# Attention units: the second bank of the even head's transposed probabilities is copied by VectorE, between the two maxima

## The chip, the cores and the metric

The kernel runs on one core of one Trainium2 chip. The metric is the device time of one launch in microseconds (us): the median of several runs. A core has TensorE (PE, and PEld for its weight loads), VectorE (DVE), ScalarE (ACT), GpSimd (POOL) and DMA queues that SyncE (SP) issues; each works through its own queue in order, and semaphores order the engines among each other.

## The reference, cut to what matters

```python
scores = scale * np.matmul(q, k.transpose(0, 1, 3, 2))      # B=2, H=8, S=576, D=64
scores = scores + bias.transpose(2, 0, 1)[None, :, :, :]
scores = scores - np.max(scores, axis=-1, keepdims=True)
attn = np.exp(scores)
attn = attn / (np.sum(attn, axis=-1, keepdims=True) + 1e-09)
return np.matmul(attn, v).astype(np.float32)
```

The bias comes from a small network over relative positions. Behind the attention stand a layer `max(x@w1, x@w2, x@w3) @ w_out` and a layer of 8 gated experts, each `max(x@w1, 0) @ w2`.

## The kernel before, in words

The kernel makes the bias first and stores it to DRAM, then does the attention, then the two layers. The change is in the attention alone.

The attention goes over 4 pairs of heads, p = 0 to 3, and in each over 9 units, k = 0 to 8: 36 units, u = 0 to 35. A unit is 128 query rows of one batch (k = 8: 64 rows of each batch) for both heads of the pair, the even head x = 0 and the odd head x = 1. All the work is issued by one hand-written loop over s = 0 to 35, and each engine takes its share in the order of that loop:

- `u_qk(s)` (lines 459 to 482): the score matmuls of unit s, into two PSUM tiles `sc`, one for each head, two banks each. The pool has two such tiles in all, so the next unit writes the same ones. The first pair multiplies unsplit inputs (line 470); the other three pairs split q and k into high and low parts and do three products (line 481), with the matmuls of the two heads in turn, the even head first. A unit with k = 8 has twice as many.
- `u_tr(s - 1, 0)` and `u_tr(s - 1, 1)` (lines 535 to 542): the transposes of the previous unit's probabilities, even head and odd head. Each goes to two PSUM tiles `pt`, one bank each: the first 64 rows to bank 0, the other 64 to bank 1. There are only these two banks, which even and odd head use in turn, so `u_tr(s - 1, 1)` waits until both banks of the even head have been copied.
- `pv_part(s)` (lines 624 to 628): matmuls of transposed probabilities with v, for units further back. Steps k = 2 and 4 of a pair have half as many again as the others.
- `u_max(s, x)` (lines 487 to 498): VectorE adds the bias to the scores of one head and takes the maximum; it shows as the instruction of line 494 with a short accumulator read behind it. It reads an `sc` tile, and so frees it.
- `u_exp(s, x)` (lines 500 to 506): ScalarE's exponential of one head.
- `u_ev(s - 1, x)` (lines 544 to 559): copies the two `pt` banks of one head to SBUF (`pts`), from where `pv_part` takes them. Before the change ScalarE (line 557) copies both banks of the even head and bank 1 of the odd head; VectorE (line 559) copies bank 0 of the odd head.
- Behind these come the pieces that only some units have: `pv_ev` and `r_add` on VectorE, and a step of weight preparation (`w_step`) at the s of `W_AT` (7 to 10, 18 to 20, 27 to 33). In the first units the loop adds spare matmuls on TensorE (`busy`, line 221).

The last unit's transposes stand behind the loop (lines 676 to 696).

Of the kernel before, what the change touches and what calls it, by code (L numbers as in the profile page):

```python
# [52 lines left out]
def make_body(stop=None):  # L53
    def body(tc, a):
# [21 lines left out]
        with ctx, tc.manual_schedule():  # L76
# [66 lines left out]
            def load_item(n):  # L143
                if n < len(w_items):
                    kind, i = w_items[n]
                    w_raw[n] = load_w64(a[f"moe_w{i % 3 + 1}"][i // 3] if kind == "w"
                                        else a["moe_w_out"][128 * i:128 * i + 128], n)
# [67 lines left out]
            def busy(p, to, n):  # L215

                q, kk = (t[:, 0] for t in qk_t[p])
                for _ in range(n):
                    for x in range(2):
                        h = slice(64 * x, 64 * x + 64)  # L220
                        T.matmul(out=to[x][:, :SH], lhsT=q[h, :128], rhs=kk[h, :SH], start=True, stop=True)
# [223 lines left out]
            with ExitStack() as actx:  # L445
# [10 lines left out]
                NP, NU = H // 2, 9 * H // 2  # L456
                un = {}

                def u_qk(u):
                    p, k = divmod(u, 9)  # L460
                    sc = [ps_s.tile([128, 2, 512], F32, tag="sc", name="sc") for _ in range(2)]
                    un[u] = {"sc": sc, "pe": []}
                    if p == 0:
                        q, kk = qk_t[p]
                        for hf in range(2):
                            for r, t in zip(half, sc):
                                to, ks = t[:, hf, :SH], slice(hf * SH, hf * SH + SH)
                                for o, b, c in ([(to, k % 2, 64 * (k % 2) + 64 * (k - k % 2))] if k < 8 else
                                                [(to[half[0]], 0, 512), (to[half[1]], 1, 0)]):
                                    T.matmul(out=o, lhsT=q[r, b, c:c + (128 if k < 8 else 64)], rhs=kk[r, b, ks],  # L470
                                             start=True, stop=True)
                        return
                    hi, lo = hl_t[p]
                    b, it = k % 2, k // 2
                    mm = [(b, 704 * b + 128 * it)] if k < 8 else [(0, 512), (1, 576)]
                    mm = [(q.rearrange("p b c -> p (b c)")[:, c:c + 128], kk[:, b]) for b, c in mm
                          for q, kk in ((hi[0], hi[1]), (hi[0], lo[1]), (lo[0], hi[1]))]
                    for hf in range(2):
                        for y, (q, kk) in enumerate(mm):
                            for x in range(2):  # L480
                                T.matmul(out=sc[x][:, hf, :SH], lhsT=q[half[x]], rhs=kk[half[x], hf * SH:hf * SH + SH],  # L481
                                         start=(y == 0), stop=(y == len(mm) - 1))
# [4 lines left out]
                def u_max(u, x):  # L487
                    p, k = divmod(u, 9)
                    ng = up.tile([128, S], F32, tag="ng", name="ng", bufs=3)
                    if k == x == 0:  # L490

                        st_t[p] = up.tile([128, 2, 18], F32, tag="st", name="st", bufs=3)
                    c = 9 * x + U_COL[k]
                    V.tensor_tensor_reduce(  # L494
                        out=ng.rearrange("p (f n) -> p f n", f=2), in0=un[u]["sc"][x][:, :, :SH],
                        in1=bias_t[2 * p + x, k // 2].rearrange("p (f n) -> p f n", f=2),
                        op0=ALU.add, op1=ALU.min, scale=-0.125, scalar=3.0e38, accum_out=st_t[p][:, 0, c:c + 1])
                    un[u]["ng", x] = ng

                def u_exp(u, x):  # L500
                    p, k = divmod(u, 9)
                    c = 9 * x + U_COL[k]
                    pe = up.tile([128, S], F32, tag="pe", name="pe", bufs=5)
                    A.activation(out=pe, in_=un[u].pop(("ng", x)), func=AF.Exp, bias=st_t[p][:, 0, c:c + 1], scale=-1.0,
                                 accum_out=st_t[p][:, 1, c:c + 1])
                    un[u]["pe"].append(pe)
# [10 lines left out]
                def r_tr(p, u):  # L517

                    T.transpose(un[u]["pt"][0][0:18, 384:512], st_t.pop(p)[:, 1, :], ident)

                def r_out(p, u):

                    A.activation(out=rt[0][0:18], in_=un[u]["pt"][0][0:18, 384:512], func=AF.Copy)
                    dma(r_d[p], rt[0][0:18])
# [10 lines left out]
                def u_tr(u, x):  # L535

                    pe = un[u]["pe"][x]
                    pt = un[u]["pt"] = [ps_t.tile([128, 512], F32, tag=f"pt{i}", name="pt") for i in range(2)]
                    for j in range(5):
                        c = min(128 * j, S - 128)  # L540
                        for i in range(2):
                            T.transpose(pt[i][:, 64 * j:64 * j + 64], pe[half[i], c:c + 128], ident[half[i], half[i]])

                def u_ev(u, x):

                    k = u % 9
                    ch = 0 if k < 4 else 1
                    to = pts[ch][:, x]
                    if k < 8:
                        c0 = CW[ch] * (k % 2) + 128 * (k // 2 % 2)  # L550
                        to = to[:, :, c0:c0 + 128].rearrange("p j (i n) -> p j i n", i=2)
                    else:
                        to = to.rearrange("p j (i n) -> p j i n", i=2)[:, :, :, 256:320]
                    for i in range(2):
                        src = un[u]["pt"][i][:, :320].rearrange("p (j n) -> p j n", n=64)
                        if x == 0 or i == 1:
                            A.activation(out=to[:, :, i], in_=src, func=AF.Copy)
                        else:
                            V.tensor_copy(out=to[:, :, i], in_=src)
# [60 lines left out]
                def in_turn(table, s):  # L620

                    return [(p, table[s - 9 * p]) for p in range(NP) if s - 9 * p in table]

                def pv_part(s):

                    for n, e in in_turn(PV, s):
                        for i in range(0, len(e), 3):
                            pv_mm(n, *e[i:i + 3])

                spare = [ps_v.tile([128, 512], F32, tag="pv", name="pv") for _ in range(2)]  # L630
                for s in range(NU):
                    p, k = divmod(s, 9)
                    u_qk(s)
                    if s > 0:
                        u_tr(s - 1, 0)
                    if s < 5:
                        busy(0, spare, 1 if s else 2)
                    pv_part(s)
                    for x in range(2):
                        u_max(s, x)  # L640
                    if s > 0:
                        u_ev(s - 1, 0)
                    u_exp(s, 0)
                    if s > 0:
                        u_tr(s - 1, 1)
                        if p > 0 and k == 1:
                            r_tr(p - 1, s - 1)
                        u_ev(s - 1, 1)
                        if p > 0 and k == 1:
                            r_out(p - 1, s - 1)  # L650
                    u_exp(s, 1)
                    for n, e in in_turn(EV, s):
                        pv_ev(n, *e)
                    if s > 8:
                        if k == 0:
                            r_add(p - 1)
                        if k in (6, 7):
                            x_out(p - 1, k - 6)
                    if s == 6:
                        start_w64(0)  # L660
                    w_step(s in W_AT, last=2)
                    if s in (3, 5):
                        load_item(s // 4)
                    if s > 0 and (k == 0 or k % 2 == 0) and 5 * p + k // 2 + 2 < 5 * NP:
                        load_bias(5 * p + k // 2 + 2)
                    if k == 2 and p > 0:
                        r_in(p - 1)
                    if k == 1:
                        load_qk(p + 1)
                    if 1 < k < 6:  # L670
                        split_qk(p + 1, k // 2 - 1, k % 2 == 1)
                    if k == 5:
                        load_v(p + 1)
                    un.pop(s - 2, None)

                u = NU - 1
# [987 lines left out]
```

## Time and profile before

| | |
|---|---|
| median of 3 runs (lowest, highest) | 1027.78 us (1027.43, 1028.0) |
| the profiled execution: time, span | 1027.61 us, 1025.8 us |
| busy share of the span: PE, DVE, ACT, POOL | 99%, 79%, 60%, 31% |
| granted TensorE clock over the span | 1.00 |
| attention units | from 62.5 to 171 us |
| copies of transposes: by ACT (L557), by DVE (L559) | 108, median 437 ns; 36, median 492 ns |
| maxima (L494), exponentials (L504) | 72, median 754 ns; 72, median 776 ns |

The span is the time from the first to the last instruction; the profiled execution's own time is 1.8 us longer. A profile row gives start and length. The ends of matmuls are modelled, and instructions of one engine overlap a little, so the distance from one start to the next says more than a length.

### The profile page before, as it was taken

How to read it: one execution, taken by the hardware profiler on the slowest of the kernel's cores; microseconds unless marked ns; L12 is line 12 of the kernel's file. 1: busy time of each engine (PE TensorE's matmuls, PEld its weight loads, DVE VectorE, ACT ScalarE, POOL GpSimd, SP SyncE). 2: the span in 40 equal slices, each digit the busy share in tenths (PEclk: the TensorE clock that was granted, in tenths of full speed). 3: DMA queues.
4: the chain of work that ended last, by engine and by line, in shares of the span. 5: the costliest groups of instructions: out<-in, count | busy, mean ns of one | idle time of the engine just before them, and what ended most of it. 6: DMA issues, size and time to landing. Idle time of an engine off the chain costs nothing.

```text
span 1025.8 us, 22004 instructions
## 1 busy us (share of the span) xinstructions
PE 1015.1 (99%) x8848; PEld 802.9 (78%) x8848; DVE 813.0 (79%) x1718; ACT 610.5 (60%) x1112; POOL 313.9 (31%) x224
## 2 busy tenths in 40 slices
PE   8999999999999999999999999999999999999998
PEld 3267777999999756478877877887887787788787
DVE  8987776899948886989778868868877977885784
ACT  9989887344326767666673565376466366536510
POOL 6961553232304111521420440341142053034100
PEclk9999999999999999999999999999999999999999
DMA  6985663433330121310310220220121022000001
GB/s 190 286 254 195 193 202 81 167 110 119 65 144 22 35 81 34 105 40 26 105 42 6 84 83 3 65 85 20 40 91 42 6 83 83 4 4 1 2 22 72
DMA packets 39459, 84.45 MB, mean 82 GB/s; under 512 B 7796, under 2 KB 10428, under 8 KB 39356
## 3 DMA queue, kind: packets, MB, share of 16 engines
q1 hardware_dynamic: 39356, 83.04, 26.2%
q8 instruction: 69, 1.13, 0.5%
q14 instruction: 34, 0.28, 0.1%
HBM read 69.73 MB, written 13.30 MB: 81 GB/s over the span
## 4 chain that ended last, share of the span: by engine, by line
PE 78%; DVE 5%; ACT 1%; issue 0%; DVEq 0%
PE x L1241 13%; PE m L602 11%; PE y L1241 9%; PE z L1241 9%; PE px L1446 7%; PE d L1344 5%; PE pz L1446 5%; PE pz L1451 5%; PE py L1446 5%; PE o L1079 4%; PE px L1451 2%; PE py L1451 2%; PE pv L571 1%; DVE hl L1264 1%; DVE P L1180 1%; ACT hh L1259 1%
## 5 line engine op out<-in xcount | busy, mean ns | idle before, releaser
L1241 PEld LDWEIGHTS <-w1h 128*128 128x128 f16 x1792 | 174.9, 98 | 45.8 <-issue 0.5
L1259 ACT ACTIVATE hh<-s 128x576 f16<-128x576 f32 x128 | 87.1, 681 | 76.9 <-DVE s L1255 49.7
L1264 DVE SCALAR_TENSOR_TENSOR hl<-s,hh 128x576 f16<-128x576 f32 x128 | 98.5, 772 | 34.1 <-ACT hh L1259 30.4
L1037 POOL TENSOR_TENSOR w2l<-w2r,w2h 128x512 f16<-128x512 f32 x56 | 65.7, 1183 | 187.7 <-ACT w2h L1036 185.4
L950 POOL TENSOR_TENSOR w1l<-wf,w1h 128x1024 f16<-128x1024 f32 x32 | 68.3, 2134 | 152.2 <-issue 85.8
L1241 PEld LDWEIGHTS <-w1l 128*128 128x128 f16 x896 | 87.7, 98 | 22.1
L944 POOL TENSOR_TENSOR w1l<-wf,w1h 128x768 f16<-128x768 f32 x32 | 53.7, 1678 | 153.8 <-ACT w1h L943 113.7
L1451 PEld LDWEIGHTS <-hh 128*128 128x128 f16 x896 | 87.7, 98 | 10.4
L1446 PEld LDWEIGHTS <-s 128*128 128x128 f16 x896 | 87.7, 98 | 10.1
L1241 PE MATMUL x<-xth,w1h 128*128 128x288 f16 x384 | 78.5, 286 | 0.0
L1241 PE MATMUL x<-xtl,w1h 128*128 128x288 f16 x384 | 78.4, 286 | 0.0
L1241 PE MATMUL x<-xth,w1l 128*128 128x288 f16 x384 | 78.4, 286 | 0.0
L1251 ACT ACTIVATE s<-x,cx 128x576 f32<-128x576 f32 x96 | 70.5, 735 | 12.2 <-PE x L1241 11.7
L1335 DVE SCALAR_TENSOR_TENSOR acc<-px,kh,acc 128x256 f32<-128x256 f32 x112 | 52.7, 480 | 29.9 <-PE px L1446 26.6
L602 PE MATMUL m<-xh,wh 128*128 128x384 f32 x216 | 73.3, 340 | 0.0
L602 PE MATMUL m<-xl,wh 128*128 128x384 f32 x216 | 73.0, 338 | 0.0
L602 PE MATMUL m<-xh,wl 128*128 128x384 f32 x216 | 73.0, 338 | 0.0
L1255 DVE SCALAR_TENSOR_TENSOR s<-z,cx,s 128x576 f32<-128x576 f32 x64 | 52.2, 816 | 24.8 <-PE z L1241 21.5
L494 DVE CUSTOM_DVE_ANT_0 ng<-sc,bias 128x576 f32<-128x576 f32 x72 | 51.6, 754 | 15.5 <-PE sc L481 7.0
L1035 ACT ACTIVATE w2r<-w2r,pc 128x512 f32<-128x512 f32 x48 | 34.0, 708 | 49.8 <-DVE pc L1021 49.8
L947 ACT ACTIVATE w1h<-wf 128x1024 f16<-128x1024 f32 x32 | 33.6, 1051 | 43.2 <-DVE wf L940 43.2
L1446 PE MATMUL px<-t,s 128*128 128x256 f16 x448 | 58.1, 273 | 0.0
(269 smaller groups left out, 2772.7 us busy)
## 6 DMA issues: line engine op xcount, KB each, us to landing
wr<-in_moe_w SPq DMA_DIRECT2D x50, 512.0 KB, 3.8
w2r<-in_moe_w SPq DMA_DIRECT2D x64, 256.0 KB, 2.9
bias_f<-bo SPq DMA_DIRECT2D x36, 295.5 KB, 4.0
bias<-bias_f SPq DMA_DIRECT2D x32, 288.0 KB, 3.5
qk<-in_qk SPq DMA_DIRECT2D x6, 576.0 KB, 4.8
wr<-in_moe_w_out SPq DMA_DIRECT2D x6, 512.0 KB, 3.3
v<-in_v SPq DMA_DIRECT2D x4, 640.0 KB, 4.9
bias<-bias_f SPq DMA_DIRECT2D x16, 144.0 KB, 5.0
```

The source lines that it names most:

```text
L602: T.matmul(out=p[:, :TG], lhsT=ws[:, 128 * c:128 * c + 128], rhs=xs[:, c, TG * g:TG * g + TG], start=(c == 0 and n == 0), stop=(c == 3 and ...
L944: G.tensor_tensor(out=lo[:, 0:3], in0=t[:, 1:4], in1=hi[:, 0:3], op=ALU.subtract)
L950: G.tensor_tensor(out=lo[:, 3:7], in0=t[:, 4:8], in1=hi[:, 3:7], op=ALU.subtract)
L1037: G.tensor_tensor(out=lo, in0=r, in1=hi, op=ALU.subtract)
L1241: T.matmul(out=ps[bank][:, s, :SH], lhsT=ws[:, i, c, :], rhs=xv[:, j, c, s * SH:s * SH + SH], start=(start and k == 0), stop=(k == 5), **kw)
L1251: A.activation(out=t, in_=src, func=AF.Identity, scale=c)
L1255: V.scalar_tensor_tensor(out=out, in0=z, scalar=scale, in1=out, op0=ALU.mult, op1=ALU.add)
L1259: A.activation(out=o, in_=src, func=AF.Relu)
L1264: V.scalar_tensor_tensor(out=l, in0=src, scalar=0.0, in1=o, op0=ALU.max, op1=ALU.subtract)
L1335: V.scalar_tensor_tensor(out=o, in0=ps, scalar=s, in1=o, op0=ALU.mult, op1=ALU.add)
L1446: T.matmul(out=out, lhsT=x[z][:, j], rhs=w[z][:, j], start=(start and j == z == 0), stop=(j == 3 and z == 1), skip_group_check=True)
L1451: T.matmul(out=out, lhsT=(ha, hb)[j // 4][0][:, j % 4, 128 * t:128 * t + 128], rhs=wh[:, j, n], start=False, stop=(j == 7), skip_group_che ...
```

## The change

In every unit but the last, bank 1 of the even head goes from ScalarE to VectorE. The calls in the loop change order, so that VectorE's copy stands between the maximum of the even head and that of the odd head. ScalarE's order stays what it was, with one copy less.

```diff
                     for i in range(2):
                         src = un[u]["pt"][i][:, :320].rearrange("p (j n) -> p j n", n=64)
-                        if x == 0 or i == 1:
+                        if i == 1 and x == 1 or x == 0 and (i == 0 or not (u < NU - 1)):
                             A.activation(out=to[:, :, i], in_=src, func=AF.Copy)
                         else:
                             V.tensor_copy(out=to[:, :, i], in_=src)
...
                     pv_part(s)
-                    for x in range(2):
-                        u_max(s, x)
+                    u_max(s, 0)
                     if s > 0:
                         u_ev(s - 1, 0)
+                    u_max(s, 1)
                     u_exp(s, 0)
                     if s > 0:
                         u_tr(s - 1, 1)
```

VectorE's queue in units 15 and 16, before the change (L494 is a maximum and its accumulator read, L559 a copy of a transposed bank; names have buffer numbers):

```order
L494 ISA ng_2393,st_2015<-sc_2363,bias_2169 128x576
L494 ISA st_2015 128x1
L494 ISA ng_2395,st_2015<-sc_2364,bias_2171 128x576
L494 ISA st_2015 128x1
L559 COPY pt320_1553<-pt_2401 128x5x64
L494 ISA ng_2454,st_2015<-sc_2424,bias_2169 128x576
L494 ISA st_2015 128x1
L494 ISA ng_2456,st_2015<-sc_2425,bias_2171 128x576
L494 ISA st_2015 128x1
L559 COPY pt320_1553<-pt_2462 128x5x64
```

And with the change:

```order
L494 ISA ng_2393,st_2015<-sc_2363,bias_2169 128x576
L494 ISA st_2015 128x1
L559 COPY pt320_1553<-pt_2378 128x5x64
L494 ISA ng_2397,st_2015<-sc_2364,bias_2171 128x576
L494 ISA st_2015 128x1
L559 COPY pt320_1553<-pt_2401 128x5x64
L494 ISA ng_2454,st_2015<-sc_2424,bias_2169 128x576
L494 ISA st_2015 128x1
L559 COPY pt320_1553<-pt_2439 128x5x64
L494 ISA ng_2458,st_2015<-sc_2425,bias_2171 128x576
L494 ISA st_2015 128x1
L559 COPY pt320_1553<-pt_2462 128x5x64
```

Each unit has one copy more, behind the maximum of the even head; the maximum of the odd head stands behind it.

TensorE's queue from the P·V matmuls of one unit of the second pair to the score matmuls of the next, before the change, with the engines whose semaphores an instruction waits for:

```order
L571 MATMUL pv<-pt_1552,v 64x256 x4
L542 MATMUL pt<-ident,pe 128x64 [waits Activation_49] x2
L542 MATMUL pt<-ident,pe 128x64 x8
L481 MATMUL sc<-kh,qh 128x288 [waits DVE_49] x2
L481 MATMUL sc<-kl,qh 128x288 x2
L481 MATMUL sc<-kh,ql 128x288 x2
```

And with the change:

```order
L571 MATMUL pv<-pt_1552,v 64x256 x4
L542 MATMUL pt<-ident,pe 128x64 [waits Activation_49]
L542 MATMUL pt<-ident,pe 128x64 [waits DVE_49]
L542 MATMUL pt<-ident,pe 128x64 x8
L481 MATMUL sc<-kh,qh 128x288
L481 MATMUL sc<-kh,qh 128x288 [waits DVE_49]
L481 MATMUL sc<-kl,qh 128x288 x2
L481 MATMUL sc<-kh,ql 128x288 x2
```

The order of TensorE's work is the same. The odd head's transposes into bank 1 now wait for VectorE, whose copy stands behind the maximum of the even head; the first score matmul therefore needs no wait of its own any more, and the second (odd head) still waits for VectorE.

## Rows read from the trace of the kernel before

**Rows 1.** Busy time by stage: us, then busy us (instructions), clock, DMA share, GB/s.
```profile
core 0: us, PE busy (x) PEld busy (x) DVE busy (x) ACT busy (x) POOL busy (x), PEclk, DMA share, GB/s
62.50:171.00 108.50, 107.93 (x1440) 78.92 (x1439) 77.82 (x202) 95.92 (x254) 47.02 (x36) 1.00 0.61 188
171.00:293.00 122.00, 122.00 (x724) 118.02 (x721) 100.94 (x180) 49.37 (x93) 28.90 (x22) 1.00 0.34 101
293.00:1000.00 707.00, 705.64 (x5707) 565.85 (x5706) 563.85 (x1182) 407.57 (x646) 188.64 (x122) 1.00 0.16 49
```

**Rows 2.** Who waited for whom, 62 to 171 us: total us, times, longest.
```profile
PEld pt L542 <- ACT pt L557: 13.1, 34, 0.5
...
PEld sc L481 <- DVE st L494: 0.7, 2, 0.4
```

**Rows 3.** Timeline of TensorE in unit 25: start us, us, engine, line.
```profile
136.81 0.40 PE L481 MATMUL sc<-kh,qh 64*128 64x288 f32 x2
...
139.14 0.52 PE L542 MATMUL pt<-ident,pe 64*128 64x64 f32 x10
139.47 0.42 PE L481 MATMUL sc<-kh,qh 64*128 64x288 f32 x2
```

**Rows 4.** Timeline of ScalarE and VectorE in unit 25.
```profile
137.07 0.44 ACT L557 ACTIVATE pt<-pt 128x320 f32<-128x320 f32 x1
...
138.00 0.76 DVE L494 CUSTOM_DVE_ANT_0 ng<-sc,bias 128x576 f32<-128x576 f32 x1 [0.47 <-PE sc L481]
...
138.21 0.77 ACT L557 ACTIVATE pt<-pt 128x320 f32<-128x320 f32 x2
...
138.68 0.76 DVE L494 CUSTOM_DVE_ANT_0 ng<-sc,bias 128x576 f32<-128x576 f32 x1
...
139.73 0.44 ACT L557 ACTIVATE pt<-pt 128x320 f32<-128x320 f32 x1
```

**Rows 5.** Timeline around units 19 and 20, all engines.
```profile
120.96 0.75 DVE L494 CUSTOM_DVE_ANT_0 ng<-sc,bias 128x576 f32<-128x576 f32 x1
...
121.34 0.18 PEld L481 LDWEIGHTS sc<-kh,qh 64*128 64x128 f32 x1
...
121.64 0.49 DVE L559 COPY pt<-pt 128x320 f32<-128x320 f32 x1
121.77 0.18 PEld L481 LDWEIGHTS sc<-kh,qh 64*128 64x128 f32 x1 [0.25 <-DVE st L494]
...
122.41 0.29 PE L481 MATMUL sc<-kh,ql 64*128 64x288 f32 x1
...
122.84 0.76 DVE L494 CUSTOM_DVE_ANT_0 ng<-sc,bias 128x576 f32<-128x576 f32 x1 [0.72 <-ACT rt L523]
```

**Rows 6.** Timeline of VectorE in units 18 and 19.
```profile
116.64 0.76 DVE L494 CUSTOM_DVE_ANT_0 ng<-sc,bias 128x576 f32<-128x576 f32 x1 [0.46 <-PE sc L481]
...
118.35 0.49 DVE L559 COPY pt<-pt 128x320 f32<-128x320 f32 x1 [0.27 <-PE pt L542]
118.76 0.68 DVE L578 COPY x<-pv 128x512 f32<-128x512 f32 x1
...
120.29 0.74 DVE L494 CUSTOM_DVE_ANT_0 ng<-sc,bias 128x576 f32<-128x576 f32 x1
```

**Rows 7.** Timeline of VectorE: the even head's maximum of units 21, 22, 23 and 26.
```profile
126.35 0.76 DVE L494 CUSTOM_DVE_ANT_0 ng<-sc,bias 128x576 f32<-128x576 f32 x1
...
129.22 0.76 DVE L494 CUSTOM_DVE_ANT_0 ng<-sc,bias 128x576 f32<-128x576 f32 x1 [0.45 <-PE sc L481]
...
132.66 0.76 DVE L494 CUSTOM_DVE_ANT_0 ng<-sc,bias 128x576 f32<-128x576 f32 x1
...
141.44 0.76 DVE L494 CUSTOM_DVE_ANT_0 ng<-sc,bias 128x576 f32<-128x576 f32 x1 [1.24 <-PE sc L481]
```

**Rows 8.** Timeline of VectorE in units 2, 3 and 9 (the first with split scores).
```profile
70.09 0.75 DVE L494 CUSTOM_DVE_ANT_0 ng<-sc,bias 128x576 f32<-128x576 f32 x1
...
72.06 0.76 DVE L494 CUSTOM_DVE_ANT_0 ng<-sc,bias 128x576 f32<-128x576 f32 x1 [0.64 <-PE sc L470]
...
89.26 0.76 DVE L494 CUSTOM_DVE_ANT_0 ng<-sc,bias 128x576 f32<-128x576 f32 x1
```

## The prediction

> **What bounds the kernel now.** I read the busy times by stage first, then the waits of the attention stage, then one ordinary unit on three engines. The 36 attention units fill the stretch from 62.5 to 171 us, some 3 us each, and TensorE is counted busy for 107.93 of its 108.50 us; behind it TensorE is busy for all of 122.00 us and then for 705.64 of 707.00 [rows 1]. So the stages behind have 1.4 us of slack in 829: what the attention stage gains or loses goes to the end of the kernel almost whole. A busy TensorE is modelled, though, so that stage has to be read by its order of events.
>
> Call Q the score matmuls of a unit, T0 and T1 the transposes of the unit before it (even and odd head), M0 and M1 the two maxima, C0 and C1 the copies of the transposes. In the list of waits, TensorE's weight loads wait 34 times, 13.1 us in all, for ScalarE's copies of transposes, and those of line 481 only 0.7 us for the maxima [rows 2]. By that list ScalarE is in the way and VectorE is not. One ordinary unit (unit 25, k = 7 of the third pair) says more. Q starts at 136.81 and the next Q at 139.47: 2.66 us [rows 3]. ScalarE goes round in 2.66 too, from the odd copy at 137.07 to that at 139.73, with no idle time shown [rows 4]. VectorE: M0 starts at 138.00, 1.19 behind Q; M1 at 138.68, 0.68 later; M1 ends at 139.44; the next Q starts 0.03 behind that [rows 3, 4]. This third circle is a real dependence: Q of the next unit writes the two score tiles that M0 and M1 read, each tile has one pair of banks, and the second Q matmul (odd head) waits for M1. So three circles have the same length here, with 0.03 us to spare on VectorE's. The waits list shows so little only because TensorE happens to be done at the same moment.
>
> That the third circle does hold TensorE is seen where M1 is late. At 121.34 the first score load goes, and the second stands until 121.77, released by the maximum that started at 120.96 and ended at 121.71; the next M0 starts at 122.84, 1.13 behind the end of M1 [rows 5]. (The profile puts the idle time ahead of that M0 down to a ScalarE copy; a score matmul that started at 122.41 and lasted 0.29 is later than any such copy, and fits.)
>
> **The change, part by part.**
> ScalarE loses 35 copies, one a unit. The two copies of an even head take 0.77 there [rows 4], so about 0.33 each goes: its circle falls to 2.33. This work pays only if ScalarE is what the rest waits for.
>
> VectorE gains 35 copies like L559 had, queued between M0 and M1. What such a copy reads is ready: T0 stands right behind Q on TensorE, and VectorE is with M0 for 0.68 us first. Its price on the queue: a copy that starts at 118.35 and lasts 0.49 is followed by the next instruction at 118.76, so 0.41 [rows 6]. From a maximum to the copy behind it: 120.96 to 121.64, 0.68, the same as from maximum to maximum [rows 5]. So M1 starts 0.68 + 0.41 behind M0, in place of 0.68. (The Trainium skill, "VectorE: DVE Perf Modes", section "The DRAIN you can't avoid", says that the next operation doesn't start until the pipe has emptied, which would make it 0.49. The rows with 0.41 differ from it, and are used; by the page the sum below would be 1.9 us larger.)
>
> What is queued behind the copy is M1, and who waits for M1 is the next Q, by the order of TensorE shown above. T1 now needs this copy for its second bank; it ends at M0 + 0.68 + 0.49 = M0 + 1.17. T1 started at 139.14, M0 + 1.14, so it moves by less than 0.1, and is through some 0.33 later [rows 3], before M1 ends at M0 + 1.85. So T1 isn't last; the second Q matmul is.
>
> The new circle: M0 to copy 0.68, copy to M1 0.41, M1 0.76, and 1.13 from its end to the next M0 (the first score matmul is out early here too, as at 121.34). Sum 2.98 in place of 2.66: **0.32 more** wherever VectorE's circle becomes the longest.
>
> Over a pair of heads (9 units, k = 0 to 8), steps from M0 to M0:
> - k5 to k6, k6 to k7, k8 to k0 are ordinary: 3 x 0.32.
> - k7 to k8, 138.00 to 141.44, is 3.44 [rows 4, 7]: a last unit has twice the score matmuls, 0.78 more ahead of M0, on the same circle. +0.32.
> - k0 to k1, 116.64 to 120.29, 3.65: VectorE's own queue (a sum of the pair before, a weight step) sets it [rows 6]. C1 waited 0.27 there for T1 at 118.35; VectorE is now free for it at 116.64 + 0.68 + 0.41 + 0.68 = 118.41. +0.1.
> - k1 to k2, 120.29 to 122.84, is 2.55 [rows 5, 6] and wholly this circle. +0.43.
> - k3 to k4, 126.35 to 129.22, is 2.87 [rows 7]. +0.11.
> - k4 to k5, 129.22 to 132.66, is 3.44 [rows 7], and k2 to k3 is like it: half as many P·V matmuls again, so TensorE sets them and 2.98 is hidden. 0.
> Sum 1.92 a pair, 5.76 for three. In the first and the last of them weight steps (units 7 to 10 and 27 to 33) already stretch several steps, and the last pair has no unit behind it: I take off 1.0, my choice, and keep 4.8.
> In the pair ahead of these (unsplit scores) M1 starts at 70.09 and ends at 70.84, and the next M0 starts at 72.06: 1.22 [rows 8]. The circle becomes 0.68 + 0.41 + 0.76 + 1.22 = 3.07. Six steps took 72.06 to 89.26 = 17.20; 6 x 3.07 = 18.4: +1.2, less 0.1 for the last, which is into the next pair. The step ahead of them (M0 0.68 ahead of 70.09, so 2.65) gets +0.4. Together 1.5.
>
> Sum: 4.8 + 1.5 = **6.3 us slower**. The profiled execution took 1027.61 us, with a span of 1025.8; that gives a span of 1032.1 and a time of 1033.9. The median is 0.17 above that run, so 1034.1.
>
> Bounds of the unknown: if the unsplit pair and the three k1-to-k2 steps hide their share, 1.5 + 0.9 goes and 3.9 is left (1031.7). If the copy costs its full 0.49 in some 23 steps that the circle sets (+1.9), and the first score matmul doesn't get out early, so that 1.19 + 0.03 stands for 1.13 in some 14 of them (+1.3), it is 9.5 (1037.3).
>
> **The rivals.**
> ScalarE is the true pacer. Then its 0.33 comes off the ordinary units, 12 in three pairs and 8 in the first: at most 20 x 0.33 = 6.6, and half of it, 3.3, if TensorE stands next: 1024.5, faster. For it: 13.1 us of waits for L557, and ScalarE without a gap. Against it: the even copies end at 138.21 + 0.77 = 138.98 and T1 starts at 139.14, 0.16 later [rows 3, 4], where a real release takes 0.06 (121.71 to 121.77 [rows 5]); so TensorE was not standing for the copy. It decides only if Q can do without M1 for another 0.41 us. The Trainium skill speaks for this rival: "TensorEngine Tiling (Array Packing)", section "PSUM Bottleneck", says to use both ScalarE and VectorE for emptying PSUM; nothing in this trace shows that it would pay here, where VectorE's queue also frees the score banks.
>
> The copy is hidden: M1 is late by 0.41 but Q isn't, TensorE keeps 2.66, and the gain on ScalarE goes nowhere: 1027.8. Against it stands the load that stood from 121.34 to 121.77.
>
> The copy is paid everywhere: each of 35 units gets 0.41, TensorE-bound ones too, if late C1 and T1 push the P·V matmuls as well: 14.4, 1042.2. For it: the circles are all tight. Against it: the 3.44 of k4 to k5 has 0.46 to spare over 2.98.
>
> **How the numbers follow.** The forecast case 0.83, the faster rival 0.06, the hidden one 0.05, the one paid everywhere 0.06. The range 1031.5 to 1037.5 is the forecast case with its bounds; some 0.8 lies in it, and what is left out is the three rivals and a little of the forecast's tails. A difference of 0.2% is 2.1 us, which 3.9 exceeds: slower 0.88, same 0.06, faster 0.06.
>
> **What would show it.** In the profile after: M0 to M1 1.09 apart in place of 0.68, with a copy between; the wait of score loads for the maxima up from 0.7 us to several; the waits of transposes for L557 down, with no gain in time; Q to Q in ordinary units 2.98, in k4 units still 3.42 to 3.44; ScalarE with about 0.6 us idle a unit; the stretch to 171 us some 6 us longer and all behind it shifted by the same. The forecast is wrong if M1 is late and Q still starts every 2.66, or if ordinary units get shorter.

## The result and the profile after

The changed kernel takes 1033.96 us in the median of 4 runs (1033.84 to 1034.44), against 1027.85 for the kernel before on the same chip (1027.43 to 1028.0): a ratio of 1.0062, with an interval of 1.005 to 1.0074. It is 6.1 us slower. The forecast was 1034.1.

First the busy times by stage, of the kernel after, in the three stages of [rows 1]; the attention stage now ends at 177 instead of 171 us.

```profile
core 0: us, PE busy (x) PEld busy (x) DVE busy (x) ACT busy (x) POOL busy (x), PEclk, DMA share, GB/s
62.50:177.00 114.50, 113.73 (x1439) 81.98 (x1439) 90.28 (x236) 89.42 (x220) 47.11 (x36) 1.00 0.60 178
177.00:299.00 122.00, 122.00 (x727) 118.02 (x722) 101.24 (x182) 49.29 (x93) 28.88 (x22) 1.00 0.35 101
299.00:1006.00 707.00, 705.66 (x5707) 565.91 (x5706) 563.75 (x1182) 407.38 (x646) 188.54 (x122) 1.00 0.16 49
```

The stages behind keep their 122 and 707 us: the first matmul of line 602 comes at 177.19 instead of 171.07, that of line 1079 at 299.08 instead of 292.96, both 6.12 later. TensorE still reads as busy all the time, 113.73 of 114.50 us: the modelled busy time has grown by 5.80 us over the same work. It says nothing of what is slow. VectorE has 34 instructions more in this stretch and 12.46 us more of busy time, ScalarE 34 fewer and 6.50 us less.

The waits between 62 and 178 us: waiting instruction, releaser, total us, times, longest.

```profile
ACT pt L557 <- PE pt L542: 16.0, 38, 1.0
...
PEld pt L542 <- ACT pt L557: 3.0, 7, 0.5
PEld sc L481 <- DVE st L494: 2.6, 14, 0.2
```

The waits of transposes for ScalarE's copies have gone from 13.1 to 3.0 us [rows 2], and the kernel is slower. The time behind that number hasn't gone: in every unit from 10 to 34 the loads of T1 stand 0.38 to 0.49 us behind those of the P·V matmuls, before and after within 0.01 of each other; only the name has changed, to "issue" in most of them (9.8 us in the same list). The waits of the score loads for the maxima have gone from 0.7 to 2.6 us, from 2 to 14 times, while the stage lost 6.1. Neither number of this list is the cost or the gain of anything; ScalarE now waits for the transposes.

An ordinary unit (unit 25, the one of [rows 3, 4]), in the timeline of all engines: start us, us, engine, line.

```profile
140.73 0.72 PE L481 MATMUL sc<-kh,qh 64*128 64x288 f32 x2
...
141.05 0.18 PEld L481 LDWEIGHTS sc<-kh,qh 64*128 64x128 f32 x1 [0.16 <-DVE st L494]
...
142.13 0.76 DVE L494 CUSTOM_DVE_ANT_0 ng<-sc,bias 128x576 f32<-128x576 f32 x1 [0.68 <-PE sc L481]
...
142.82 0.49 DVE L559 COPY pt<-pt 128x320 f32<-128x320 f32 x1
...
143.22 0.75 DVE L494 CUSTOM_DVE_ANT_0 ng<-sc,bias 128x576 f32<-128x576 f32 x1
143.36 0.39 PEld L542 LDWEIGHTS pt<-ident,pe 64*128 64x128 f32 x10 [0.38 <-issue]
...
143.70 0.73 PE L481 MATMUL sc<-kh,qh 64*128 64x288 f32 x2
...
144.03 0.18 PEld L481 LDWEIGHTS sc<-kh,qh 64*128 64x128 f32 x1 [0.17 <-DVE st L494]
```

This is the new circle, row by row. M0 starts at 142.13; the copy 0.69 later; M1 at 143.22, 1.09 behind M0. T1 goes at 143.36, before M1 is through, and the first score matmul (even head) at 143.70. The load for the odd head stands until 144.03, 0.06 behind the end of M1 at 143.97. Q to Q is 2.97 us in place of 2.66 [rows 3]. Of the 0.41 that M1 is later, 0.10 is hidden: the even head's first score matmul, which stands ahead of the odd head's, is out 0.27 ahead of the end of M1 and runs beside it; before, it came 0.03 behind that end [rows 3, 4].

In the unsplit pair, the same timeline around units 2 and 3:

```profile
70.39 0.75 DVE L494 CUSTOM_DVE_ANT_0 ng<-sc,bias 128x576 f32<-128x576 f32 x1
...
70.84 1.36 PE L470 MATMUL sc<-qk 64*128 64x288 f32 x7
...
72.17 0.76 DVE L494 CUSTOM_DVE_ANT_0 ng<-sc,bias 128x576 f32<-128x576 f32 x1 [0.62 <-PE sc L470]
```

M1 runs from 70.39 to 71.14, and the first score matmul is out at 70.84, 0.30 ahead of that end. From the end of M1 to the next M0 it is 1.03 us, where before it was 1.22 [rows 8].

The steps from M0 to M0, taken from the starts of the maxima in both traces (us; k is the unit's place in its pair, the three split pairs in a row). The steps of the first row are called light below.

| step | before | after | difference | forecast |
|---|---|---|---|---|
| k5-k6, k6-k7, k8-k0 (second and third pair) | 2.65 to 2.69 | 2.96 to 2.98 | +0.27 to +0.34 | +0.32 |
| k7-k8 | 3.44, 3.44, 3.46 | 4.14, 3.76, 3.76 | +0.70, +0.32, +0.30 | +0.32 |
| k0-k1 | 3.11, 3.65, 3.38 | 3.19, 3.73, 3.47 | +0.08, +0.08, +0.09 | +0.1 |
| k1-k2 | 3.00, 2.55, 2.56 | 3.10, 3.07, 3.06 | +0.10, +0.52, +0.50 | +0.43 |
| k2-k3 | 3.50, 3.51, 3.50 | 3.49, 3.49, 3.49 | -0.01 to -0.02 | 0 |
| k3-k4 | 2.87, 2.87, 3.06 | 2.96, 2.97, 2.97 | +0.09, +0.10, -0.09 | +0.11 |
| k4-k5 | 3.44, 3.44, 3.97 | 3.50, 3.50, 3.96 | +0.06, +0.06, -0.01 | 0 |
| unsplit pair and into the next, M0 of unit 2 to M0 of unit 9 | 19.86 | 20.81 | +0.95 | +1.5 |

In the last pair k5-k6 goes from 2.55 to 2.96, and k6-k7 from 2.87, already stretched by a weight step, to 2.98. From Q to Q the k4 units now have 3.58 to 3.59 (forecast 3.42 to 3.44), since their own first score matmul goes early and the next one doesn't; their M0 to M0 is in the table. M0 of unit 35 is 6.02 us later than before; the span ends 6.1 us later.

### The profile page after: what moved, and what is told of

Read it like the earlier page. It is cut to its first block, busy times and chain, and to the rows that moved or that the text cites. A ratio compares the mean times of both kernels' runs of the same rounds, so it can differ in the third digit from the quotient of the medians.

```text
span 1031.9 us, 21980 instructions
## 1 busy us (share of the span) xinstructions
PE 1021.3 (99%) x8848; PEld 806.1 (78%) x8848; DVE 825.7 (80%) x1753; ACT 603.6 (58%) x1077; POOL 313.8 (30%) x224
## 3 DMA queue, kind: packets, MB, share of 16 engines
q8 instruction: 69, 1.13, 0.5%
## 4 chain that ended last, share of the span: by engine, by line
PE 78%; DVE 5%; ACT 1%; issue 0%; DVEq 0%
PE x L1241 13%; PE m L602 11%; PE y L1241 9%; PE z L1241 9%; PE px L1446 7%; PE d L1344 5%; PE py L1446 5%; PE pz L1451 5%; PE pz L1446 5%; PE o L1079 4%; PE px L1451 2%; PE py L1451 2%; PE pv L571 1%; DVE hl L1264 1%; DVE P L1180 1%; ACT hh L1259 1%
## 5 line engine op out<-in xcount | busy, mean ns | idle before, releaser
L494 DVE CUSTOM_DVE_ANT_0 ng<-sc,bias 128x576 f32<-128x576 f32 x72 | 54.0, 751 | 18.3 <-PE sc L481 7.4
L504 ACT ACTIVATE pe<-ng,st 128x576 f32<-128x576 f32 x72 | 55.5, 771 | 5.6 <-DVE st L494 3.6
```

What stands on the lines that cost most here:

```text
L494: V.tensor_tensor_reduce(out=ng.rearrange("p (f n) -> p f n", f=2), in0=un[u]["sc"][x][:, :, :SH], in1=bias_t[2 * p + x, k // 2].rearrange ...
```

## Experiments

Each was run beside the kernel before on the same chip; the ratio is to that kernel's runs there.

**Behind both maxima.** The copies are those of the change, in the loop order of before, so that VectorE's new copy stands behind M1. M1 isn't late, and T1 is.

```diff
-                        if x == 0 or i == 1:
+                        if i == 1 and x == 1 or x == 0 and (i == 0 or not (u < NU - 1)):
```

> The changed kernel's copies, but VectorE's copy of the even head queued behind both maxima, as the loop stood before. Theory A (the second score matmul waits for the odd head's maximum, and the odd head's transposes for the copy): the maximum is early again, but the copy now ends 0.68 + 0.68 + 0.49 = 1.85 us behind the start of the even maximum, the transposes are through some 0.4 us later, and the next even maximum comes 1.19 behind that: 3.42 a step in place of 2.66 before and 2.97 after. About +16 us over before, so 1044. Theory B (35 copies more on VectorE cost what they cost, wherever they stand): as the changed kernel, 1034. Theory C (only the place between the maxima hurts): 1027.8.

Measured: 1049.07 us, ratio 1.0206 (1.0191 to 1.0221). The light steps are 3.35 to 3.36 but for one of 3.72, and the steps k0-k1 and k1-k2 of the third pair 4.34 and 3.74, in place of 3.65 and 2.55. Timeline of all engines in one light unit:

```profile
151.73 0.76 DVE L494 CUSTOM_DVE_ANT_0 ng<-sc,bias 128x576 f32<-128x576 f32 x1 [0.46 <-PE sc L481]
...
153.09 0.49 DVE L559 COPY pt<-pt 128x320 f32<-128x320 f32 x1
...
153.63 0.46 PE L542 MATMUL pt<-ident,pe 64*128 64x64 f32 x8 [0.48 <-DVE pt L559]
...
153.91 0.38 PE L481 MATMUL sc<-kh,qh 64*128 64x288 f32 x1
```

And from its list of waits, 62 to 193 us:

```profile
PEld pt L542 <- DVE pt L559: 21.1, 29, 2.1
```

Here the copy is on the path itself: it ends at 153.58, T1 goes on at 153.63, and Q at 153.91, which stands behind T1 on TensorE. The wait is in the list this time, 21.1 us. So the place in the queue decides: the same copies cost 6.1 us between the maxima and 21.3 behind them. The size was forecast too small (1044). The expectation doesn't share its 16 us out by steps, so which of them it undervalued isn't known; the steps k0-k1 and k1-k2, where VectorE has its extra pieces, lost 0.7 and 1.2 us in the third pair and 5.1 us in the three split pairs together.

**ScalarE with a copy less, VectorE unchanged.** In units 9 to 34 nobody makes the copy.

```diff
-                    for i in range(2):
+                    for i in range(1 if x == 0 and 9 <= u < NU - 1 else 2):
```

> The kernel before, with bank 1 of the even head not copied by any engine in units 9 to 34 (later units reuse what the first pair left there, so the output is not the reference's). Theory A: ScalarE was not what the rest waited for, so the time stays at 1027.8, within 0.7 us. Rival (ScalarE was the pacer, 0.33 us less for it in each ordinary unit): 12 to 26 units x 0.33 = 4 to 8.6 us less, 1019 to 1024.

Measured: 1027.12 us, ratio 0.9993 (0.9984 to 1.0002). Timeline of all engines from M0 of unit 24 to M0 of unit 25:

```profile
135.75 0.76 DVE L494 CUSTOM_DVE_ANT_0 ng<-sc,bias 128x576 f32<-128x576 f32 x1 [0.45 <-DMA bias<-bias_f]
...
135.90 1.08 PE L571 MATMUL pv<-pt,v 128*64 128x256 f32 x8
135.98 0.44 ACT L557 ACTIVATE pt<-pt 128x320 f32<-128x320 f32 x1
...
136.91 0.39 PEld L542 LDWEIGHTS pt<-ident,pe 64*128 64x128 f32 x10 [0.39 <-issue]
...
137.51 0.44 ACT L557 ACTIVATE pt<-pt 128x320 f32<-128x320 f32 x1
...
138.43 0.76 DVE L494 CUSTOM_DVE_ANT_0 ng<-sc,bias 128x576 f32<-128x576 f32 x1 [0.47 <-PE sc L481]
```

And before the change, in unit 25:

```profile
138.13 1.08 PE L571 MATMUL pv<-pt,v 128*64 128x256 f32 x8
...
139.14 0.39 PEld L542 LDWEIGHTS pt<-ident,pe 64*128 64x128 f32 x10 [0.38 <-ACT pt L557]
```

ScalarE makes one copy of the even head, T1's weight loads now wait 0.39 us for "issue" instead of 0.38 for L557, and M0 to M0 is 2.68 as before. Over the 36 units the light steps stay at 2.65 to 2.69; the step k1-k2 of the first split pair gained 0.22 and two steps of the last pair 0.11 and 0.12. ScalarE isn't the pacer of an ordinary unit, and the 13.1 us are time in which the loads of T1 stood anyway: they go 1.01 us behind the first P·V matmul with the copy (138.13 to 139.14) and without it (135.90 to 136.91), and in every unit from 10 to 34 their idle time is the same within 0.01.

**An add between the maxima, before's copies.** VectorE adds two small SBUF tiles (128x320, their data of no use) between M0 and M1, for s > 0. M1 is as late as after the change, and nothing waits for the add itself.

```diff
-                    for x in range(2):
-                        u_max(s, x)
+                    u_max(s, 0)
+                    if s > 0:
+                        V.tensor_tensor(out=dj[1], in0=dj[0], in1=dj[0], op=ALU.add)
+                    u_max(s, 1)
```

> The kernel before (all its copies unchanged), with an addition of 128x320 elements on VectorE between the two maxima of units 1 to 35, from SBUF to SBUF, which nothing waits for. Theory A: it delays the odd head's maximum by some 0.41 us and so costs what the change cost, about +6 us: 1033 to 1034.5. Rival (the cost of the change is the wait of the odd head's transposes for VectorE's copy): no transposes wait here, 1027.8.

Measured: 1042.18 us, ratio 1.0139 (1.0124 to 1.0154), more than twice the cost that was expected. The add's line in the trace (ns: shortest, median, longest), and timeline in the first split pair:

```profile
L643 DVE TENSOR_TENSOR jk<-jk x35: 479/489/1729, 66.8 to 184.9; 128x320 f32<-128x320 f32 x35
```

```profile
101.87 1.16 POOL L63 TENSOR_SCALAR qh<-qk 128x1152 fp32r<-128x1152 f32 x1 [24.43 <-DMA qk<-in_qk]
...
102.00 1.36 DVE L643 TENSOR_TENSOR jk<-jk 128x320 f32<-128x320 f32 x1
...
103.28 0.74 DVE L494 CUSTOM_DVE_ANT_0 ng<-sc,bias 128x576 f32<-128x576 f32 x1
```

The usual add lasts 0.49, this one 1.36: it starts while a GpSimd instruction runs (101.87 to 103.03) and ends 0.33 behind it. Ten of the 35 adds are over 0.55, all of them beside a GpSimd instruction, and all 35 together last 24.52 us, 7.4 more than 35 times the median. Where the add isn't held, the light steps are 2.96 to 2.98. So this run doesn't price M1's lateness, because its own instrument was disturbed; the next but one repeats it with an instruction that isn't.

**The copy between the maxima, another one back to ScalarE.** As the change, but the odd head's bank 0 goes back from VectorE to ScalarE: VectorE and ScalarE have as many copies as before, and only the place on VectorE is new.

```diff
-                        if i == 1 and x == 1 or x == 0 and (i == 0 or not (u < NU - 1)):
+                        if x == 1 or i == 0 or not (u < NU - 1):
```

> The changed kernel, but bank 0 of the odd head goes back to ScalarE: VectorE has as many copies as before the change and ScalarE too, only VectorE's stands between the maxima. Theory A: the place is what costs: about 1034, up to 1 us more since ScalarE now makes both odd copies. Theory B (the amount of work on VectorE): 1027.8.

Measured: 1033.2 us, ratio 1.0051 (1.0035 to 1.0068). Timeline of VectorE, M0 of unit 24 to M0 of unit 25:

```profile
138.92 0.76 DVE L494 CUSTOM_DVE_ANT_0 ng<-sc,bias 128x576 f32<-128x576 f32 x1 [1.13 <-ACT pt L557]
...
139.60 0.48 DVE L559 COPY pt<-pt 128x320 f32<-128x320 f32 x1
140.00 0.75 DVE L494 CUSTOM_DVE_ANT_0 ng<-sc,bias 128x576 f32<-128x576 f32 x1
...
141.90 0.76 DVE L494 CUSTOM_DVE_ANT_0 ng<-sc,bias 128x576 f32<-128x576 f32 x1 [1.14 <-PE sc L481]
```

VectorE now stands idle for 1.14 us ahead of the second M0, and the step is 2.98 all the same. It isn't the amount of VectorE's work that costs, but what stands ahead of M1. The heavier steps moved: k0-k1 is 0.24 to 0.36 shorter than before (VectorE has no copy behind M1 there any more), and k1-k2 0.41 to 0.69 longer.

**A reduction between the maxima, before's copies.** As the add, with an instruction that has one input (it reads 128x320 and writes one column).

```diff
-                    for x in range(2):
-                        u_max(s, x)
+                    u_max(s, 0)
+                    if s > 0:
+                        V.tensor_reduce(out=dj[1][:, 0:1], in_=dj[0], op=ALU.max, axis=AX.X)
+                    u_max(s, 1)
```

> As the addition between the maxima, but the idle instruction is a maximum over 320 elements (one SBUF input, one output column), some 0.40 us on VectorE's queue. In the run with the addition, that instruction lasted 0.49 us in most units but up to 1.73 us, always beside a GpSimd operation. Theory A with that correction (the place between the maxima costs 0.41; the rest of that run's 14.4 us was the addition held up beside GpSimd): +5.5 to +6.5, 1033 to 1034.5. Rival (any instruction there costs 14 us, so the change gained some 8 us elsewhere): 1042.

Measured: 1034.15 us, ratio 1.0061 (1.0046 to 1.0076); the change itself has 1.0062. The reduction's line:

```profile
L643 DVE TENSOR_REDUCE jk<-jk x35: 475/481/482, 67.2 to 177.2; 128x1 f32<-128x320 f32 x35
```

It is never held (475 to 482 ns), and light steps are 2.96 to 2.98, those of the change. Nobody waits for the reduction, and ScalarE makes all its old copies; M1's lateness by itself brings the same loss as the change. What the 0.33 us that the change saves on ScalarE in each unit is worth can't be told from nothing beside it. Two steps of the last pair, k2-k3 and k4-k5, are longer here than after the change (3.86 and 4.55, there 3.49 and 3.96): in the second of them the weight step's L131 lasts 1.28 us beside a GpSimd instruction, against 0.68.

**Twice the delay.** The change, and that reduction behind the new copy and ahead of M1.

```diff
                     if s > 0:
                         u_ev(s - 1, 0)
+                        V.tensor_reduce(out=dj[1][:, 0:1], in_=dj[0], op=ALU.max, axis=AX.X)
                     u_max(s, 1)
```

> The changed kernel with a second instruction between the maxima (a maximum over 320 SBUF elements, some 0.40 us, which nothing waits for). Theory A: the circle of VectorE grows from 2.97 to 3.37 us; 7 of 9 steps in each of three pairs and 7 in the first get 0.40 more, the two steps that TensorE sets (3.44 to 3.5) get nearly none: about +11 us over the changed kernel, 1045 (1043 to 1047). If the bound changed to another engine meanwhile, less.

Measured: 1043.37 us, ratio 1.0153 (1.0139 to 1.0167). Timeline of VectorE in a light unit:

```profile
145.18 0.76 DVE L494 CUSTOM_DVE_ANT_0 ng<-sc,bias 128x576 f32<-128x576 f32 x1 [0.71 <-ACT pe L504]
...
145.86 0.49 DVE L559 COPY pt<-pt 128x320 f32<-128x320 f32 x1
146.26 0.47 DVE L644 TENSOR_REDUCE jk<-jk 128x1 f32<-128x320 f32 x1
146.66 0.75 DVE L494 CUSTOM_DVE_ANT_0 ng<-sc,bias 128x576 f32<-128x576 f32 x1
...
148.55 0.76 DVE L494 CUSTOM_DVE_ANT_0 ng<-sc,bias 128x576 f32<-128x576 f32 x1 [0.74 <-PE sc L481]
```

The step is 3.37, and the light steps are 3.35 to 3.38: another 0.40 on the circle's 2.97, the price of one instruction on VectorE's queue. The steps k2-k3 and k4-k5 of the third pair, 3.50 and 3.52, still hide it. Over the kernel with the change it is +9.4 us, a little below what was expected (some 11), while the change itself was 6.1: in the light steps the first 0.41 had 0.1 of cover, the second none. 0.9 of the 9.4 is the step k4-k5 of the last pair alone, where L131 lasted 1.60 us beside a GpSimd instruction, against 0.68.

**The change in six units only.** VectorE takes the copy in the loop steps k = 2 and 4 of the split pairs, which the prediction says are held by TensorE; the loop order is that of the change.

```diff
-                        if i == 1 and x == 1 or x == 0 and (i == 0 or not (u < NU - 1)):
+                        if i == 1 and x == 1 or x == 0 and (i == 0 or not (u > 8 and u % 9 in (1, 3))):
```

> The change in 6 units alone: VectorE copies bank 1 of the even head only where k = 2 or 4 of the second to fourth pair, the steps with half as many P.V matmuls again. Theory A: there the odd head's maximum ends some 0.8 us ahead of the next scores, so 0.41 is hidden, and what ScalarE is spared gains nothing: 1027.8, within 0.5. Theory B (each copy costs where it stands): 6 x 0.41 = 2.5 more, 1030.3.

Measured: 1027.93 us, ratio 1.0003 (0.9994 to 1.0012). Timeline of VectorE in unit 22, with all engines:

```profile
129.14 0.76 DVE L494 CUSTOM_DVE_ANT_0 ng<-sc,bias 128x576 f32<-128x576 f32 x1 [0.45 <-PE sc L481]
...
129.83 0.48 DVE L559 COPY pt<-pt 128x320 f32<-128x320 f32 x1
130.23 0.75 DVE L494 CUSTOM_DVE_ANT_0 ng<-sc,bias 128x576 f32<-128x576 f32 x1
...
132.59 0.76 DVE L494 CUSTOM_DVE_ANT_0 ng<-sc,bias 128x576 f32<-128x576 f32 x1
```

M1 is 0.41 later here too, and the step is 3.45 against 3.44 before [rows 7]. Five of the six steps are within 0.01 us of those before: there the copy is free, since TensorE's own work makes the unit longer than VectorE's circle. The sixth (unit 31, in the last pair) has 4.30 against 3.97, with L131 at 1.15 us beside a GpSimd instruction against 0.83, and the step behind it 2.91 against 2.55, of which the next gives 0.28 back.

**Can anything be gained on the same path?** Two kernels tried to shorten VectorE's queue in the steps k0-k1, which it holds [rows 6]. The first moves three weight steps of the kernel before from k = 0 and 1 to k = 6 and 7:

```diff
-W_AT = (7, 8, 9, 10, 18, 19, 20, 27, 28, 29, 30, 31, 32, 33)
+W_AT = (7, 8, 9, 10, 15, 19, 20, 24, 25, 29, 30, 31, 32, 33)
```

> The kernel before, with three VectorE steps of weight preparation moved: that of unit 18 to unit 15, those of units 27 and 28 to units 24 and 25. Theory A (VectorE's queue and then its circle set the steps from k = 0 to k = 2): 3.65 and 3.38 us from maximum to maximum become about 3.1, 0.8 us in all, of which the new places cost 0.1 to 0.2: 1027.1 (1026.9 to 1027.5). If TensorE alone sets the stage: 1027.8.

Measured: 1028.38 us, ratio 1.0007 (0.9998 to 1.0016) where 1027.1 us had been expected. The steps k0-k1 shrank as forecast, to 3.11 both (-0.54 and -0.27), and k1-k2 gave back 0.23 each. What undid the rest was the moved step in unit 15, in the timeline of all engines:

```profile
109.92 1.43 POOL L588 TENSOR_TENSOR xl<-x,xh 128x576 fp32r<-128x576 f32 x1
...
110.42 1.48 DVE L131 SCALAR_TENSOR_TENSOR ww<-wr,ww 128x512 int32<-128x512 int32 x1
```

In its old place (unit 18) it lasted 0.63; here it starts beside a GpSimd instruction and ends 0.55 behind it, and the step from unit 15 to 16 went from 2.68 to 3.53.

The second takes the opposite direction from the change, in four units: the odd head's bank 0 goes from VectorE to ScalarE.

```diff
-                        if x == 0 or i == 1:
+                        if x == 0 or i == 1 or u in (8, 17, 26, 30):
```

> The opposite move, at four places: the kernel before, with VectorE's own copy (bank 0 of the odd head) given to ScalarE where VectorE's queue sets the step, in the passes s = 9, 18, 27 and 31. In the run with the place changed and the amount kept, the steps from there to the next even maximum were 0.24, 0.36, 0.36 and 0.35 us shorter. Theory A: these come out again; the step behind (k = 1 to k = 2) then meets TensorE's 2.78 in place of 2.55 and gives back up to 0.23 in two of them: 0.8 to 1.1 us in all, 1026.5 to 1027.0. Theory B (ScalarE is the pacer, 0.33 more for it at four places): 1027.8 to 1029.1.

Measured: 1028.15 us, ratio 1.0004 (0.9995 to 1.0013), where a gain had been expected (1026.5 to 1027.0). Timeline of all engines in units 18 to 20:

```profile
117.01 0.76 DVE L494 CUSTOM_DVE_ANT_0 ng<-sc,bias 128x576 f32<-128x576 f32 x1 [0.46 <-PE sc L481]
...
118.73 0.77 ACT L557 ACTIVATE pt<-pt 128x320 f32<-128x320 f32 x2
...
119.55 0.39 PEld L542 LDWEIGHTS pt<-ident,pe 64*128 64x128 f32 x9 [0.16 <-ACT pt L557]
119.91 0.74 DVE L494 CUSTOM_DVE_ANT_0 ng<-sc,bias 128x576 f32<-128x576 f32 x1
...
121.23 0.52 PE L542 MATMUL pt<-ident,pe 64*128 64x64 f32 x10
...
121.89 0.40 PE L481 MATMUL sc<-kh,qh 64*128 64x288 f32 x2
...
123.08 0.76 DVE L494 CUSTOM_DVE_ANT_0 ng<-sc,bias 128x576 f32<-128x576 f32 x1 [0.58 <-PE sc L481]
```

M0 of unit 19 comes after 2.90 instead of 3.65 us, and M0 of unit 20 after 3.17 more instead of 2.55: 6.07 for both, before 6.20, a gain of 0.13. VectorE is early now and TensorE isn't. T0's loads stand until 119.55 for the odd head's second copy, which ScalarE ends at 119.50; the P·V matmuls, T1 at 121.23 and Q at 121.89 follow from there, and M1, over at 121.33, holds nobody. Counted from M0 of unit 18, Q is even later than before, 4.88 against 4.70. In the other three places even that is missing: 6.37 against 6.11 and 6.06 against 5.94 for the two steps of the other pairs, and of 0.38 gained at unit 31, 0.46 was lost two steps later. Neither of the two kernels is faster than before by a difference that can be told from none.

## Why the prediction was right

**The mechanism.** In the changed kernel VectorE's circle, through the odd head's score banks, holds the light units. An instruction that nobody waits for and that makes M1 as late (the reduction) gives 1.0061, the change 1.0062. In the trace after, the odd head's score load starts 0.06 us behind the end of M1 in 20 of the 27 steps from unit 8 on; in the six k2 and k4 units it is 0.45 to 0.47, in unit 10 0.13. ScalarE didn't hold them before the change either: taking a copy off it alone, in units 9 to 34, gives 0.9993. There VectorE's circle was no longer than the others: from k5 to k8 of the second and third pair the even head's score load came 0.00 to 0.04 behind the end of M1, in TensorE's own order, and the odd head's 0.06. That VectorE alone held these units then, so that a shorter circle would have gained there, isn't shown. The list of waits had pointed at ScalarE, and the order of starts in one unit was right: three circles of the same length, of which one was made longer.

**The light step.** Forecast 2.98, measured 2.96 to 2.98, with the terms as they were put: M0 to copy 0.69 (0.68), copy to M1 0.40 (0.41), and 1.13 to 1.15 from the end of M1 to the next M0 (1.13). The rule of the Trainium skill in "VectorE: DVE Perf Modes", section "The DRAIN you can't avoid", that was weighed there would have made the copy 0.49; the row of after, from 142.82 to 143.22, has 0.40. The prediction read only half of that section, which goes on that a next operation that isn't held starts earlier; with that the 0.40 and 0.41 agree.

**The heavier steps.** k2-k3 and k4-k5 hide the copy, as forecast, but for 0.06 in two of the k4-k5 steps, and the six-unit kernel shows it by itself in five of its six steps (1.0003). k0-k1 +0.1 and k3-k4 +0.11 came as 0.08 to 0.09 and 0.09 to 0.10, but for the last pair's k3-k4, which a weight step had stretched to 3.06 and which became 0.09 shorter. ScalarE's idle time in unit 25 is 0.37 us in two waits (0.22 and 0.15), below the 0.6 named. k1-k2, forecast +0.43, came at 0.50 and 0.52 in two pairs and at 0.10 in the first split pair, whose step was 3.00 already.

**The unsplit pair, mis-sized.** The term was 1.5 us. From M0 of unit 2 to M0 of unit 9 it measured 0.95; the step into unit 2 is 0.12 shorter, and M0 of unit 9 comes 0.86 later than before. The prediction took over 1.22 for the way from the end of M1 to the next M0; with M1 late, the first score matmul is out ahead of its end in units 2, 3, 4 and 6, and 1.01 to 1.04 is left (steps of 2.85 to 2.87). In units 5 and 7 (3.20 each) it comes 0.05 and 0.13 behind that end, so VectorE doesn't hold them. The prediction had used the early matmul for the split pairs, not here.

**The split pairs.** Forecast 5.76, less a deduction of 1.0, so 4.8; measured 5.16. The deduction was about the right size (0.33 in the first split pair's k1-k2, 0.64 in the last pair's light steps and its k3-k4), and k7-k8 of the first split pair brought 0.38 more than its like. M0 of unit 17 starts 0.68 us behind the start of the last score matmul, that of unit 26 0.30. Timeline of VectorE there, with all engines:

```profile
116.45 0.76 DVE L494 CUSTOM_DVE_ANT_0 ng<-sc,bias 128x576 f32<-128x576 f32 x1 [1.86 <-PE pt L542]
```

The row puts it down to transposes, which this maximum doesn't read. Two kernels with the same order ahead of M1, the one with another copy back on ScalarE and the one with the reduction, have 3.79 and 3.78 for this step, not 4.14. What held M0 stays open; it is one unit of one profile.

**The whole.** 0.86 + 5.16 = 6.02 at M0 of unit 35, 6.1 at the end. That it came so near to 6.3 has some luck in it: the first pair was 0.6 too large, the others 0.4 too small, and most of that 0.4 is the one step of unit 17. All of it passed to the end, as the busy times by stage had said. The rival of a copy paid everywhere fell with the heavy steps; the hidden one with the load that stands until 144.03. The prediction's lower bound takes 0.9 for the three k1-k2 steps, where three times 0.43 is 1.3, and so lies some 0.4 too high; nothing else hangs on it.

## What to carry to other kernels

Before work is moved to an engine with idle time, ask what stands behind the new place in that engine's queue, and which buffer it frees: the same copies cost 6 us ahead of M1 and 21 us behind it, and six of them, in units that TensorE holds, nothing that could be told from none. Where several circles have the same length, the list of waits can put idle time down to an engine that nobody stands for; measure each one's slack from starts in one unit, and take work off one of them alone before believing it the bound. And a circle made longer is not the sum of its parts: the place where it comes back in (here the first score matmul, early by 0.3 us) may have slack that only appears when something else is late.

## What the runs showed of the hardware

An add on VectorE of two tiles in SBUF took 0.49 us by itself, and up to 1.73 where a GpSimd instruction was running; the weight step's integer instruction (L131), also with two SBUF inputs, went from 0.63 with no GpSimd instruction beside it to 1.48 with one. The reduction, with one SBUF input, stayed at 475 to 482 ns through all 35 units, in 18 of them beside a GpSimd instruction. This agrees with what the Trainium skill states in "SBUF — State Buffer", section "Who interferes with whom": a VectorE instruction with two SBUF inputs contends with a GpSimd instruction that reads SBUF, and a reduction never does on this chip. This contention was the main reason why two of the expectations missed (those of the add and of the moved weight steps), and it makes such an add useless as a delay of known length.
